# A 64-step stretch of a fused attention and ELU feed-forward kernel: all three engines put in program order, and five instead of three early groups

## The chip, the cores and the metric

The kernel runs on one core of a Trainium2 chip. The metric is device time in microseconds (us) of one execution. The profile is of one execution of its own, by the hardware profiler; its times are microseconds from the start of its span.

## What is computed

Four batches of channel attention over 6080 rows and 256 channels, followed by a feed-forward layer with an ELU over all 24320 rows. Both weights come as 64-bit floats.

```python
def _attn_ref(q, k, v, tau):                       # B, N, C = 4, 6080, 256
    qn = q / (np.linalg.norm(q, axis=1, keepdims=True) + 1e-06)
    kn = k / (np.linalg.norm(k, axis=1, keepdims=True) + 1e-06)
    s = kn.transpose(0, 2, 1) @ qn / tau
    s = s - s.max(-1, keepdims=True)
    a = np.exp(s)
    a /= a.sum(-1, keepdims=True) + 1e-09
    return (v @ a).astype(np.float32)

def _moe_ref(x, w_in, w_out):                      # x: 24320 x 256, d_ff 2048
    h = x @ w_in
    g = np.where(h > 0.0, h, np.exp(np.minimum(h, 0.0)) - 1.0)
    return (g @ w_out).astype(np.float32)
```

## The kernel before

**Stages.** The attention matrix of a batch is only 256 x 256, so the kernel multiplies it into `w_in` first: `wp` = a x `w_in`, kept as a rounded part (hi) and a remainder (lo), and then works on v alone. For batch 0, q and k are read in 24 groups of two rows for each of 128 partitions; TensorE sums their product (`gram`, in full 32-bit precision), ScalarE squares them and VectorE adds the squares (`acc`). Then come the norms (`norms0`, the tile `pn`), the spread of one norm over the partitions (`dg`, a matmul), the softmax, the transposes (`pt`, `aT`) and the projection (`pw`, then `wp`) of the first quarter of `w_in`, in two halves of 256 columns for each of two channel tiles.

**Steps.** After that the kernel goes through steps. A step is one chunk of 512 rows of v (`vt`, or `scr_r` for chunks 2 and 3) and one block of 128 of the 2048 hidden columns. Step i computes `ph`, six matmuls of 512 columns (three for each of two channel tiles: hi x hi, hi x lo, lo x hi); ScalarE makes relu and exp of it, VectorE the ELU (`e`); one step later ScalarE casts it to `g` and VectorE takes the remainder; three steps later six matmuls add it into the output (`po`). The first 64 steps take chunks 0 to 3 in turns of four blocks, so that a quarter of the weights is enough to begin: while they run, the rest of `w_in` and `w_out` is converted from 64-bit floats and the rest of `wp` is projected. After step 64 each chunk has its 16 steps in a row, and the gram products of batches 1 to 3 stand between the output matmuls of these steps, in hi and lo parts.

**Conversion.** `to_f32` is a generator that turns a piece of 64-bit weights into 32-bit ones: one ScalarE operation (Abs) and six on VectorE, with a yield after nearly each. `converting_w_in` does so for `w_in` (into `wf`), `converting_w_out` for `w_out` (into `cv`, then a ScalarE cast and a VectorE remainder into `wo`). A table of steps (`convert`, the list `loose`) says at which step each piece between two yields is issued; `splits` says at which steps the two halves of a chunk of v are cast and split (the list `side`).

**Early groups.** The first `EARLY` = 3 groups of batch 1 are loaded ahead and their gram product is summed in full precision into the PSUM tile `pe` while the softmax of batch 0 runs (`early_items`); the later pass over batch 1 leaves their product out.

**Order.** A scheduler sets the order of each engine's instructions by priorities, but not inside `manual_schedule`, where the named engines take them as the program is written. Before, that holds for TensorE and the DMA queue of SP up to the first step, and for VectorE in the steps up to 66 (64 and three more). ScalarE's order is the scheduler's throughout, and so is TensorE's in the steps. Three PSUM buffers (`w`) go round among `pn`, `pt`, `pw` and `ph`, so a new one waits until the third before it has been read.

## Time and profile before

| what | value |
|---|---|
| median of 3 runs | 2177.08 us (2177.03 to 2178.02) |
| the profiled execution | 2178.38 us, of it the profiled span 2176.6 us |
| TensorE busy | 2165.8 us, 10220 records |
| VectorE busy | 1524.3 us, 2354 records |
| ScalarE busy | 1468.8 us, 2416 records |

A busy time is the sum of an engine's records. TensorE's records overlap one another, so that a full-looking TensorE can still be waiting between two starts; what it loses is read from the starts. A full-precision matmul shows as two records.

### The profile page before, as it was taken

What the parts mean: (1) busy time and instruction counts of PE and PEld (TensorE: products, weight loads), DVE (VectorE), ACT (ScalarE), POOL (GpSimd) and SP (SyncE); (2) the same over time, 40 slices, a digit from 0 to 9 for tenths busy, and PEclk for the clock granted to TensorE, in tenths of its full rate; (3) what the DMA queues carried; (4) which work ended last, traced back from release to release, by engine and by line L of the source; (5) the groups of instructions that cost most, each with busy time, mean ns of one, the idle gap of its engine ahead of it and who ended that gap; (6) DMA issues with size and microseconds to landing.
All of it is one profiled execution on the core that took longest, in us unless ns stands there. A gap on an engine that the chain in (4) does not pass through costs nothing.

```text
span 2176.6 us, 27102 instructions
## 1 busy us (share of the span) xinstructions
PE 2165.8 (100%) x10220; PEld 1907.5 (88%) x10220; DVE 1524.3 (70%) x2354; ACT 1468.8 (67%) x2416; POOL 3.3 (0%) x11
## 2 busy tenths in 40 slices
PE   9999999999999999999999999999999999999999
PEld 8788888898888888889888888888988888888998
DVE  6887777777866777667776667676777666666665
ACT  6876776766767666666676666666676666666665
POOL 0000000000000000000000000000000000000000
PEclk9999999999999999999999999999999999999999
DMA  9310222221201111111021111121112000000000
GB/s 336 126 59 20 78 68 68 68 66 49 61 27 59 59 49 59 49 58 55 30 68 39 49 49 59 49 67 49 46 39 67 21 20 29 29 20 10 20 10 20
DMA packets 61956, 119.73 MB, mean 55 GB/s; under 512 B 6144, under 2 KB 16000, under 8 KB 61824
## 3 DMA queue, kind: packets, MB, share of 16 engines
q1 hardware_dynamic: 61680, 117.86, 16.4%
q8 instruction: 80, 1.31, 0.3%
q14 instruction: 52, 0.43, 0.1%
q10 hardware_dynamic: 144, 0.13, 0.0%
HBM read 90.96 MB, written 27.00 MB: 54 GB/s over the span
## 4 chain that ended last, share of the span: by engine, by line
PE 97%; DVE 1%; ACT 1%; DMA 0%; issue 0%; SPq 0%; DVEq 0%
PE po L431 15%; PE po L433 15%; PE po L429 15%; PE ph L391 15%; PE ph L392 15%; PE ph L393 15%; PE gram L203 3%; PE gram L517 2%; PE gram L210 1%; PE pw L349 0%; PE pw L351 0%; PE pw L350 0%; PE pw L346 0%; ACT e L403 0%; DMA wi<-in_moe_w_in_dram 0%
## 5 line engine op out<-in xcount | busy, mean ns | idle before, releaser
L112 ACT CAST g<-e 128x512 fp32r<-128x512 f32 (+1 forms) x768 | 470.3, 613 | 521.5 <-DVE e L408 285.1
L113 DVE TENSOR_TENSOR g<-e,g 128x512 fp32r<-128x512 f32 (+1 forms) x768 | 525.5, 684 | 325.8 <-ACT g L112 293.1
L429 PE MATMUL po<-g,wo 128*128 128x512 f32 (+1 forms) x1536 | 578.9, 377 | 0.7 <-ACT wo L489 0.7
L431 PE MATMUL po<-g,wo 128*128 128x512 f32 (+1 forms) x1536 | 579.3, 377 | 0.0
L433 PE MATMUL po<-g,wo 128*128 128x512 f32 (+1 forms) x1536 | 577.5, 377 | 0.0
L391 PE MATMUL ph<-vt,wp 128*128 128x512 f32 (+1 forms) x1472 | 556.5, 378 | 1.5 <-DVE e L404 1.5
L392 PE MATMUL ph<-vt,wp 128*128 128x512 f32 (+1 forms) x1472 | 554.6, 377 | 0.1
L393 PE MATMUL ph<-vt,wp 128*128 128x512 f32 (+1 forms) x1472 | 554.5, 377 | 0.0
L404 DVE SCALAR_TENSOR_TENSOR e<-e,ph 128x512 f32<-128x512 f32 (+1 forms) x416 | 283.4, 681 | 251.5 <-ACT e L403 250.1
L429 PEld LDWEIGHTS po<-g,wo 128*128 128x128 f32 x1536 | 290.2, 189 | 39.1 <-ACT wo L489 1.1
L431 PEld LDWEIGHTS po<-g,wo 128*128 128x128 f32 x1536 | 290.3, 189 | 38.1 <-DVE wo L491 0.4
L433 PEld LDWEIGHTS po<-g,wo 128*128 128x128 f32 x1536 | 290.4, 189 | 34.8 <-DVE g L113 0.5
L402 ACT ACTIVATE e<-ph 128x512 f32<-128x512 f32 (+1 forms) x416 | 246.3, 592 | 98.6 <-PE ph L393 83.4
L391 PEld LDWEIGHTS ph<-vt,wp 128*128 128x128 f32 x1472 | 278.2, 189 | 39.6 <-DVE e L404 3.1
L392 PEld LDWEIGHTS ph<-vt,wp 128*128 128x128 f32 x1472 | 278.2, 189 | 36.9 <-issue 0.5
L393 PEld LDWEIGHTS ph<-vt,wp 128*128 128x128 f32 x1472 | 278.2, 189 | 36.0
L403 ACT ACTIVATE e<-e 128x512 f32<-128x512 f32 (+1 forms) x416 | 260.9, 627 | 12.2
L408 DVE TENSOR_TENSOR e<-ph,e 128x512 f32<-128x512 f32 (+1 forms) x352 | 240.9, 685 | 10.4
L406 ACT ACTIVATE e<-ph 128x512 f32<-128x512 f32 (+1 forms) x352 | 207.7, 590 | 30.8 <-PE ph L393 27.3
L407 DVE TENSOR_SCALAR e<-e 128x512 f32<-128x512 f32 (+1 forms) x352 | 147.2, 418 | 21.2 <-ACT e L406 20.9
L182 DVE TENSOR_TENSOR acc<-acc,sq 128x1024 f32<-128x1024 f32 x84 | 102.6, 1221 | 12.6 <-ACT sq L181 11.5
L203 PE MATMUL gram<-qk 128*128 128x512 f32 x276 | 104.6, 379 | 0.0
(120 smaller groups left out, 1170.4 us busy)
## 6 DMA issues: line engine op xcount, KB each, us to landing
raw<-in_q_dram SPq DMA_DIRECT2D x76, 256.0 KB, 2.7
raw<-in_k_dram SPq DMA_DIRECT2D x76, 256.0 KB, 2.9
v<-in_v_dram SPq DMA_DIRECT2D x32, 512.0 KB, 3.6
out_dram<-o SPq DMA_DIRECT2D x56, 256.0 KB, 2.0
v<-in_v_dram SPq DMA_DIRECT2D x16, 496.0 KB, 3.6
out_dram<-o SPq DMA_DIRECT2D x31, 248.0 KB, 2.1
wraw<-w_scr SPq DMA_DIRECT2D x12, 512.0 KB, 3.2
room<-in_q_dram SPq DMA_DIRECT2D x16, 256.0 KB, 5.2
```

The lines of the kernel that those rows point to most:

```text
L112: nc.scalar.copy(hi, src)
L113: nc.vector.tensor_sub(lo, src, hi.bitcast(F32))
L391: nc.tensor.matmul(ph[:, 0:n], wp[kt][:, 0, fs], hi, start=(kt == 0), stop=False)
L392: nc.tensor.matmul(ph[:, 0:n], wp[kt][:, 0, fs], lo, start=False, stop=False)
L393: nc.tensor.matmul(ph[:, 0:n], wp[kt][:, 1, fs], hi, start=False, stop=(kt == KT - 1))
L402: nc.scalar.activation(ev, pv, AF.Relu, scale=-1.0)
L403: x = nc.scalar.activation(ev, ev, AF.Exp, scale=-1.0)
L404: y = nc.vector.scalar_tensor_tensor(ev, ev, -1.0, pv, op0=ALU.add, op1=ALU.max)
L408: y = nc.vector.tensor_tensor(ev, pv, ev, op=ALU.max)
L429: nc.tensor.matmul(o, wo[:, f, 0, ds], hi, start=first(c, f), stop=False)
L431: nc.tensor.matmul(o, wo[:, f, 1, ds], hi, start=False, stop=False)
L433: nc.tensor.matmul(o, wo[:, f, 0, ds], lo, start=False, stop=last(c, f))
```

## The change

1. `EARLY` goes from 3 to 5. Group 3 lies in the fourth quarter of the scratch tile, group 4 in a `raw` buffer of its own; both are loaded on SP's queue between the second load of v and the second load of `w_in`. Their matmuls are not issued before the first step but inside steps 0, 1 and 2, and the copy of `pe` moves to step 3.
2. VectorE is in program order from the norms on, with conversions issued at fixed places in the norms and in the softmax (`meanwhile`); ScalarE from the transposes on. In the softmax of batch 0 ScalarE, not VectorE, scales the gram product.
3. The conversions of the first four rows of `w_out`, and the cast of chunk 1, are spread over the four projections and the first five steps.
4. The first 67 steps run in program order on TensorE and ScalarE as well as VectorE. The tables of conversions and splits change; `converting_w_out` yields once more, so its last piece comes a step later at one place.

```diff
     LEFT = N - RP * P
-    EARLY = 3
+    EARLY = 5
...
-    def inverse_norms(y, ry, squares):
+    def inverse_norms(y, ry, squares, meanwhile=None):
         root = nc.scalar.activation(y, squares, AF.Sqrt)
+        if meanwhile is not None:
+            meanwhile()
         nc.vector.tensor_scalar(ry, y, 1e-30, None, op0=ALU.max)
...
-    def softmax(b, gram, rq, rk, nm):
         for ct in range(KT):
             r = rk[:, ct : ct + 1]
             if b == 0:
-                nc.vector.tensor_scalar(a[:, ct], gram[ct][:, 0, :], r, None, op0=ALU.mult)
+                nc.scalar.activation(a[:, ct], gram[ct][:, 0, :], AF.Copy, scale=r)
...
+        if meanwhile is not None:
+            meanwhile()
         nc.vector.tensor_scalar(sm, sm, 1e-9, None, op0=ALU.add)
         done = nc.vector.reciprocal(sm, sm)
...
+    def split_v_hi(c, raw, vt, kt):
+        n = span(c)[2]
+        nc.scalar.copy(vt[:, kt, 0, 0:n], raw[:, kt, 0:n])
+
+    def split_v_lo(c, raw, vt, kt):
+        n = span(c)[2]
+        nc.vector.tensor_sub(vt[:, kt, 1, 0:n], raw[:, kt, 0:n], vt[:, kt, 0, 0:n].bitcast(F32))
+
     def split_v(c, raw, vt, kt):
-        n = span(c)[2]
-        split(vt[:, kt, 0, 0:n], vt[:, kt, 1, 0:n], raw[:, kt, 0:n])
+        split_v_hi(c, raw, vt, kt)
+        split_v_lo(c, raw, vt, kt)
...
     def converting_w_out(t, n):
-        for of in to_f32(wo64[t // FS][:, t % FS : t % FS + n].rearrange("p t (d x) -> p t d x", x=2)):
-            if of is None:
-                yield
+        if t % FS == 0:
+            state["cv"] = work.tile([P, FS, D], F32, tag="cv", bufs=1, name="cv")
+        ts = slice(t % FS, t % FS + n)
+        of = state["cv"][:, ts]
+        yield from to_f32(wo64[t // FS][:, ts].rearrange("p t (d x) -> p t d x", x=2), of)
         nc.scalar.copy(wo[:, t : t + n, 0], of)
         yield
         nc.vector.tensor_sub(wo[:, t : t + n, 1], of, wo[:, t : t + n, 0].bitcast(F32))
...
-        raw1 = [scratch(x, k=2 * 2).rearrange("p (t r) c -> p t r c", t=2) for x in range(EARLY)]
+        raw1 = [scratch(x, k=2 * 2).rearrange("p (t r) c -> p t r c", t=2) for x in range(M)]
...
         vraw[0] = load_v(0)
-        for x in range(EARLY):
+        for x in range(EARLY - 2):
             fill_rows(raw1[x], 1, x)
         wo64[0] = load_w_out(0)
+        parts = [converting_w_in(0, slice(x * CH // 2, (x + 1) * CH // 2)) for x in range(2)]
+
+        def go_on(part, n):
+            for _ in range(n):
+                next(part, None)
+
         for x in range(FULL - BEHIND, FULL):
             if x == FULL - 2:
-                pn, dg, rk, nm = norms0(acc)
-                with tc.issue_after(summed[0]), tc.issue_after(summed[1]):
-                    at_once(converting_w_in(0, slice(0, CH // 2)))
+                with tc.issue_after(summed[0]), tc.issue_after(summed[1]), tc.manual_schedule(engines={nc.vector.engine}):
+                    go_on(parts[0], 1)
+                    pn, dg, rk, nm = norms0(acc, lambda: go_on(parts[0], 1))
+                    go_on(parts[0], 2)
             gram0_item(x)
         pe = ps.tile([P, KT, C], F32, tag="o", bufs=8 - KT - WB, name="pe")
         spread(pn, dg)
         vraw[1] = load_v(1)
+        raw1.append(work.tile([P, 2, 2, C], F32, tag="raw", bufs=5, name="raw_early"))
+        for x in range(EARLY - 2, EARLY):
+            fill_rows(raw1[x], 1, x)
         wi64[1] = load_w_in(1)
         wo64[1] = load_w_out(1)
-        a0, rs0, attended = softmax(0, pg0, pn[:, 1, :], rk, nm)
-        vts[0] = new_vt(0)
-        with tc.issue_after(attended):
+        wps[0] = new_wp(0)
+        first_w_out, second_w_out = converting_w_out(0, 2), converting_w_out(2, 2)
+
+        def meanwhile():
+            go_on(parts[0], 2)
+            go_on(parts[1], 2)
+
+        with tc.manual_schedule(engines={nc.vector.engine}):
+            a0, rs0, attended = softmax(0, pg0, pn[:, 1, :], rk, nm, meanwhile)
+            vts[0], vts[1] = new_vt(0), new_vt(1)
+            at_once(parts[1])
             for kt in range(KT):
                 split_v(0, vraw[0], vts[0], kt)
             del vraw[0]
-        early_items(4)
-        wps[0] = new_wp(0)
-        aT0, copied = transpose_a(0, a0)
-        attended = (attended, copied)
-        early_items(2 * EARLY - 4)
-        for part in range(2):
-            for ct in range(KT):
-                wp_item(aT0, rs0, wf[0], wps[0], ct, 0, part, 2)
+            early_items(4)
+            with tc.manual_schedule(engines={nc.scalar.engine}):
+                aT0, copied = transpose_a(0, a0)
+                go_on(first_w_out, 2)
+                early_items(2)
+                attended = (attended, copied)
+
+                between = [
+                    lambda: (split_v_hi(1, vraw[1], vts[1], 0), go_on(first_w_out, 1)),
+                    lambda: (split_v_hi(1, vraw[1], vts[1], 1), go_on(first_w_out, 1)),
+                    lambda: (go_on(second_w_out, 1), go_on(first_w_out, 1)),
+                    lambda: go_on(first_w_out, 1),
+                ]
+                for part in range(2):
+                    for ct in range(KT):
+                        wp_item(aT0, rs0, wf[0], wps[0], ct, 0, part, 2)
+                        between[part * KT + ct]()
     nc.sync.dma_start(w_scr[0], wf[0])
     vraw[2] = load_v(2)
-    with tc.issue_after(attended[0]), tc.issue_after(attended[1]):
-        with tc.manual_schedule(engines={nc.vector.engine}):
-            at_once(converting_w_out(0, 2))
-        nc.scalar.copy(early, pe)
...
-    convert(converting_w_out(2, 2), (1, 2, 3, 3, 4, 4, 4), (wi64, 2, load_w_in))
-    convert(converting_w_in(1), (4, 5, 7, 8, 9, 10), (wi64, 3, load_w_in))
-    convert(converting_w_out(4, 4), (11, 12, 13, 14, 15, 16, 17), (wo64, 2, load_w_out))
+
+    for step, n in ((0, 2), (1, 1), (2, 1)):
+        at(step, lambda n=n: early_items(n), True)
+    at(3, lambda: nc.scalar.copy(early, pe), True)
+    convert(first_w_out, (0, 0))
+    convert(second_w_out, (1, 2, 2, 3, 3, 4, 4), (wi64, 2, load_w_in))
+    convert(converting_w_in(1), (1, 5, 6, 8, 8, 10), (wi64, 3, load_w_in))
+    convert(converting_w_out(4, 4), (11, 12, 13, 14, 15, 16, 17, 18), (wo64, 2, load_w_out))
     convert(converting_w_in(2), (18, 19, 20, 21, 22, 23), (wo64, 3, load_w_out))
-    convert(converting_w_out(8, 4), (23, 24, 25, 27, 28, 31, 32))
+    convert(converting_w_out(8, 4), (23, 24, 25, 27, 28, 31, 32, 33))
     convert(converting_w_in(3), (32, 33, 34, 35, 36, 37))
-    convert(converting_w_out(12, 4), (38, 39, 40, 41, 43, 44, 47))
+    convert(converting_w_out(12, 4), (38, 39, 40, 41, 43, 44, 45, 47))
...
-    splits = [(1, 1, 2), (2, 6, 6), (3, 9, 11)]
+    splits = [(1, 0, 1), (2, 5, 7), (3, 9, 11)]
     def prep(x, kt):
         c = splits[x][0]
-        if kt == 0:
-            vts[c] = new_vt(c)
-        split_v(c, vraw[c], vts[c], kt)
+        if c == 1:
+            split_v_lo(c, vraw[c], vts[c], kt)
+        else:
+            if kt == 0:
+                vts[c] = new_vt(c)
+            split_v(c, vraw[c], vts[c], kt)
...
     done = []
-    with tc.manual_schedule(engines={nc.vector.engine}):
+    with tc.manual_schedule(engines={nc.tensor.engine, nc.vector.engine, nc.scalar.engine}):
         for i in range(M * FT + LAG):
             take(i)
```

VectorE between the softmax and the first step. The rows lead from the second half of `wf_0` to the `wp` remainders of two of the four projections; `cv` belongs to `w_out`. Before:

```order
L133 SCALAR_TENSOR_TENSOR wf_0_340<-wi64_0_237,wf_0_340 128x2x256
L129 TENSOR_SCALAR cv_438<-cv_438 128x512
L138 TENSOR_SCALAR cv_s_382<-wf_0_340 128x512
L131 TENSOR_SCALAR cv_438<-cv_438 128x512
L141 SCALAR_TENSOR_TENSOR cv_s_382<-wi64_0_237,cv_s_382 128x512
L133 SCALAR_TENSOR_TENSOR cv_438<-wo64_0_304,cv_438 128x512
L143 TENSOR_TENSOR wf_0_340<-wf_0_340,cv_s_382 128x2x256
L358 SCALAR_TENSOR_TENSOR wp_0_0_398<-pw_412,sums_366,wp_0_0_398 128x256
L358 SCALAR_TENSOR_TENSOR wp_0_1_399<-pw_417,sums_366,wp_0_1_399 128x256
```

And now:

```order
L131 SCALAR_TENSOR_TENSOR wf_0_320<-wi64_0_237,wf_0_320 128x2x256
L136 TENSOR_SCALAR cv_s_395<-wf_0_320 128x512
L139 SCALAR_TENSOR_TENSOR cv_s_395<-wi64_0_237,cv_s_395 128x512
L141 TENSOR_TENSOR wf_0_320<-wf_0_320,cv_s_395 128x2x256
L386 TENSOR_TENSOR vt_0_392<-v_0_296,vt_0_392 128x512 x2
L127 TENSOR_SCALAR cv_421<-cv_421 128x512
L129 TENSOR_SCALAR cv_421<-cv_421 128x512
L360 SCALAR_TENSOR_TENSOR wp_0_0_371<-pw_429,sums_376,wp_0_0_371 128x256
L131 SCALAR_TENSOR_TENSOR cv_421<-wo64_0_304,cv_421 128x512
L360 SCALAR_TENSOR_TENSOR wp_0_1_372<-pw_436,sums_376,wp_0_1_372 128x256
```

The second half of `wf_0` now ends ahead of everything that belongs to `cv`, and the two halves of `vt` stand behind it; the `wp` remainders have conversion pieces of `cv` between them.

VectorE around steps 3 and 4, with the second piece of `w_out` (`cv`) on its way to `wo`. Before:

```order
L133 SCALAR_TENSOR_TENSOR cv_478<-wo64_0_304,cv_478 128x512
L138 TENSOR_SCALAR cv_s_524<-cv_478 128x512
L404 SCALAR_TENSOR_TENSOR e_533<-e_533,ph_526 128x512
L113 TENSOR_TENSOR g_537<-e_508,g_537 128x512
L141 SCALAR_TENSOR_TENSOR cv_s_524<-wo64_0_304,cv_s_524 128x512
L143 TENSOR_TENSOR cv_478<-cv_478,cv_s_524 128x512
L491 TENSOR_TENSOR wo_81<-cv_478,wo_81 128x2x256
```

And now, where `e_530` is step 3 and `e_555` step 4:

```order
L131 SCALAR_TENSOR_TENSOR cv_421<-wo64_0_304,cv_421 128x512
L136 TENSOR_SCALAR cv_s_521<-cv_421 128x512
L414 SCALAR_TENSOR_TENSOR e_530<-e_530,ph_523 128x512
L113 TENSOR_TENSOR g_534<-e_511,g_534 128x512
L139 SCALAR_TENSOR_TENSOR cv_s_521<-wo64_0_304,cv_s_521 128x512
L141 TENSOR_TENSOR cv_421<-cv_421,cv_s_521 128x512
L414 SCALAR_TENSOR_TENSOR e_555<-e_555,ph_548 128x512
L113 TENSOR_TENSOR g_559<-e_530,g_559 128x512
L503 TENSOR_TENSOR wo_81<-cv_421,wo_81 128x2x256
```

The last two pieces of the conversion used to be followed at once by the remainder into `wo`; now a step's `e` and `g` stand between.

ScalarE around step 11, with chunk 3's second half (`scr_r`). Before:

```order
L402 ACTIVATE e_704<-ph_697 128x512
L403 ACTIVATE e_704<-e_704 128x512
L112 CAST g_708<-e_679 128x512
L112 CAST scr_r_86<-v_3_602 128x512
L112 CAST g_736<-e_704 128x512
L127 ACTIVATE wf_3_1216<-wi64_3_695 128x1024
L402 ACTIVATE e_732<-ph_725 128x512
L402 ACTIVATE e_754<-ph_747 128x512
L403 ACTIVATE e_732<-e_732 128x512
```

And now, where the first row is the relu of step 11 and the sixth that of step 12:

```order
L412 ACTIVATE e_722<-ph_715 128x512
L413 ACTIVATE e_722<-e_722 128x512
L112 CAST g_726<-e_697 128x512
L125 ACTIVATE cv_737<-wo64_1_369 128x1024
L382 CAST scr_r_86<-v_3_643 128x512
L412 ACTIVATE e_750<-ph_743 128x512
L413 ACTIVATE e_750<-e_750 128x512
```

The cast of the chunk's half used to follow the cast of `g` at once; now the Abs of the next rows of `w_out` is ahead of it. The conversion of `wf_3`, which stood ahead of two relus, is gone from this place, and relu and exp of a step stand together.

## Rows read from the trace of the kernel before

**Rows 1.** Two stretches: length; busy us of PE, PEld, DVE, ACT, POOL; granted clock; DMA.

```profile
46.00:105.50 59.50, 54.52 (x234) 42.27 (x233) 48.82 (x91) 45.64 (x82) 0.00 (x0) 1.00 0.38 133
105.50:2170.00 2064.50, 2064.45 (x9783) 1825.06 (x9784) 1444.48 (x2234) 1392.54 (x2303) 2.10 (x3) 1.00 0.14 46
```

**Rows 2.** Timeline of TensorE: start, length, line, operation, count, idle before.

```profile
46.03 3.70 PE L517 MATMUL gram<-raw 128*128 128x256 f32 x16
...
50.29 0.70 PE L279 MATMUL pn<-dg,ones 128*128 128x256 f32 x2 [0.56 <-DVE dg L257]
...
60.91 0.57 PE L391 MATMUL ph<-vt,wp 128*128 128x512 f32 x1
...
67.36 0.42 PE L429 MATMUL po<-g,wo 128*128 128x512 f32 x1
...
105.56 0.48 PE L391 MATMUL ph<-scr_r,wp 128*128 128x512 f32 x1 [0.36 <-DVE wp L358]
...
108.25 0.38 PE L391 MATMUL ph<-scr_r,wp 128*128 128x512 f32 x1
...
110.84 0.38 PE L391 MATMUL ph<-scr_r,wp 128*128 128x512 f32 x1
```

**Rows 3.** Timeline of TensorE in the later pass over batch 1.

```profile
285.08 0.38 PE L203 MATMUL gram<-qk 128*128 128x512 f32 x1
285.30 0.38 PE L431 MATMUL po<-g,wo 128*128 128x512 f32 x1
285.51 0.27 PE L210 MATMUL gram<-qk 128*128 128x256 f32 x1
285.62 0.38 PE L433 MATMUL po<-g,wo 128*128 128x512 f32 x1
```

**Rows 4.** Timeline of VectorE ahead of step 0, and one later row.

```profile
51.27 0.74 DVE L300 TENSOR_TENSOR a<-a,pn 128x256 f32<-128x256 f32 x2
...
51.93 0.74 DVE L301 TENSOR_REDUCE nm<-a 128x1 f32<-128x256 f32 x2
...
56.59 0.42 DVE L138 TENSOR_SCALAR cv_s<-wf 128x512 uint32<-128x512 uint32 x1
...
57.26 0.69 DVE L141 SCALAR_TENSOR_TENSOR cv_s<-wi,cv_s 128x512 f32<-128x512 uint32 x1
...
59.06 0.87 DVE L358 SCALAR_TENSOR_TENSOR wp<-pw,sums,wp 128x256 fp32r<-128x256 f32 x2
...
114.86 1.22 DVE L491 TENSOR_TENSOR wo<-cv,wo 128x1024 fp32r<-128x1024 f32 x1
```

**Rows 5.** Timeline of all engines in one step after 106.7 us.

```profile
106.74 0.38 PE L393 MATMUL ph<-scr_r,wp 128*128 128x512 f32 x1
...
107.15 0.60 ACT L402 ACTIVATE e<-ph 128x512 f32<-128x512 f32 x1 [0.41 <-PE ph L393]
...
107.78 0.64 ACT L403 ACTIVATE e<-e 128x512 f32<-128x512 f32 x1
...
108.45 0.69 DVE L404 SCALAR_TENSOR_TENSOR e<-e,ph 128x512 f32<-128x512 f32 x1 [0.49 <-ACT e L403]
...
109.06 0.68 DVE L113 TENSOR_TENSOR g<-e,g 128x512 fp32r<-128x512 f32 x1
```

**Rows 6.** Timeline of ScalarE between 83 and 89 us.

```profile
83.46 1.61 ACT L127 ACTIVATE wf<-wi 128x1024 f32<-128x1024 f32 x1
...
84.95 0.63 ACT L112 CAST g<-e 128x512 fp32r<-128x512 f32 x1
...
87.26 0.63 ACT L403 ACTIVATE e<-e 128x512 f32<-128x512 f32 x1
...
87.80 0.61 ACT L112 CAST g<-e 128x512 fp32r<-128x512 f32 x1
...
88.31 0.61 ACT L112 CAST scr_r<-v 128x512 fp32r<-128x512 f32 x1
```

**Rows 7.** Timeline of SP's DMA queue: the second load of w_in.

```profile
41.39 0.37 SPq L467 DMA_DIRECT2D wi<-in_moe_w_in_dram  x1
```

More of the change, by code (lines that the diff above doesn't have):

```diff
@@ L113, in split, with to_f32 @@
         nc.vector.tensor_sub(lo, src, hi.bitcast(F32))
-    def to_f32(pair, dst=None):
+    def to_f32(pair, dst):
         low, high = pair[:, :, :, 0], pair[:, :, :, 1]
         shape = list(low.shape)
-        if dst is None:
-            dst = work.tile(shape, F32, tag="cv", bufs=1, name="cv")
         af, a = dst, dst.bitcast(U32)
@@ L237, in inverse_norms, with norms0 @@
         return nm
-    def norms0(acc):
+    def norms0(acc, meanwhile):
         pn = ps.tile([P, 2, C], F32, tag="w", bufs=WB, name="pn")
@@ L253, in norms0 @@
         y, ry = (tiny.tile([P, W], F32, name=f"{x}0") for x in ("y", "ry"))
-        nm = inverse_norms(y, ry, pn[:, 0, 0:W])
+        nm = inverse_norms(y, ry, pn[:, 0, 0:W], meanwhile)
         dg = tiny.tile([P, KT, P], F32, tag="y", bufs=1, name="dg")
@@ L279, in spread, with softmax @@
         nc.tensor.matmul(pn[:, 1, :], ones, dg.rearrange("p t j -> p (t j)"), start=True, stop=True)
-    def softmax(b, gram, rq, rk, nm):
+    def softmax(b, gram, rq, rk, nm, meanwhile=None):
         a = work.tile([P, KT, C], F32, tag="a", bufs=1, name=f"a_{b}")
@@ L512, in channel_attention_then_elu_ffn @@
     wi64, wo64, vraw, vts = {}, {}, {}, {}
+    state = {}
     def multiply(raw, r, gram, first, last):
@@ L603, in channel_attention_then_elu_ffn @@
         vraw[1] = load_v(1)
+        raw1.append(work.tile([P, 2, 2, C], F32, tag="raw", bufs=5, name="raw_early"))
+        for x in range(EARLY - 2, EARLY):
+            fill_rows(raw1[x], 1, x)
         wi64[1] = load_w_in(1)
         wo64[1] = load_w_out(1)
-        a0, rs0, attended = softmax(0, pg0, pn[:, 1, :], rk, nm)
-        vts[0] = new_vt(0)
-        with tc.issue_after(attended):
-            at_once(converting_w_in(0, slice(CH // 2, CH)))
+        wps[0] = new_wp(0)
[7 more added lines that the diff above has]
+            at_once(parts[1])
             for kt in range(KT):
@@ L644, in at @@
         (loose if free else side).setdefault(step, []).append(fn)
-    state = {}
     def fetch(w64, x, load):
```

## The prediction, made before the changed kernel ran

> **What bounds the kernel now.** I read the stretches first: busy time of each engine before, in and after the part that the change touches. From 105.50 us to 2170 us TensorE is busy all the time but 0.1 us, at granted clock 1.00 (its upper level, 2.4 GHz), while VectorE and ScalarE are free for 30 to 33% of it [rows 1]. After 105.5 us a removed matmul shortens the run and nothing else does. Before that point TensorE waits. How much is read from starts, not from busy time, because a matmul's record overlaps the next one: the twelve 512-column matmuls of one step take 108.25 to 110.84, so 2.59/12 = 0.2157 us each, though each record shows 0.38 [rows 2]. A full-precision matmul of 256 columns is two such records, 0.43 us: sixteen records last 3.70 us, of which about 0.25 us is the tail of the last, so 3.45 [rows 2].
>
> With these prices I subtract work from time. From 46.03 (the last two groups of batch 0) to 60.91 (the first matmul of step 0) the work is 3.45 for the groups, 0.43 to spread the norms, 3.45 + 1.72 for three early groups, 0.44 for four transposes and 3.45 for four half-width projections: 12.94 of 14.88 us, 1.94 lost. From 60.91 to 67.36 (step 0's output matmul) 24 matmuls, 5.18 of 6.45: 1.27 lost. From 67.36 to 105.56 (step 15) 138 matmuls, 29.77, and four full-precision projections of 0.86, 3.45: 33.2 of 38.2 us, 5.0 lost [rows 2]. So 8.2 us is the most that order can give back, 0.38% of the run.
>
> **The change, term by term.** I write P(i) for the start of the last `ph` matmul of step i.
>
> *More early groups.* Two groups of batch 1 move from the interleaved pass to the early one: eight full-precision matmuls are added, 8 x 0.43 = 3.45 us. Eight of 512 and eight of 256 columns go away from the pass after step 64; there the 512 ones start 0.22 before the next instruction and the 256 ones 0.11 [rows 3], so 4 x 0.216 + 4 x 0.108 = 1.295 per group, **2.59 us off**, in a stretch where TensorE never waits. By themselves the groups cost 0.86 us; they pay only as far as they fill waits. Their four loads of 256 KB stand on SP's queue ahead of the second `wi` load, issued at 41.39 so far [rows 7]; it is first used after step 1, near 66 us. I cost that at nothing; that cover is some ten microseconds.
>
> *Up to step 0.* VectorE now makes the norms without conversions in between, so TensorE no longer waits for `dg`: spread can follow the last gram matmul at about 49.5 and end, as long as its row, near 50.1 (before: 50.29 + 0.70) [rows 2]. The multiply and reduction pairs that took 51.27 to 52.67 [rows 4] end near 51.6; the scaling, moved to ScalarE, lies beside the spread. But VectorE then has a row of conversions ahead of the first `wp` remainder: the end of the first half of `wf`, all of its second half, two remainders of `vt`, two steps of `cv`. They are five of about 0.7, two remainders of 0.6, five short ones of 0.34 to 0.46 and the two tiny ones of `sums` (0.34 for both), by the spacing of the same kinds of rows (0.34 from 56.59 to the next, 0.60 for the long ones, 0.1 more where one needs the one just before) [rows 4]: 7.0 us. So the first `wp` remainder starts at 58.6. It frees the PSUM buffer that the fourth projection needs, at 59.15, and the next remainder, one conversion step later, ends near 60.2 and frees that of step 0. The first step starts at 60.2 instead of 60.91: **0.7 off**.
>
> *Steps 0 to 3.* The early matmuls stand between the `ph` groups: 24 x 0.2157 + 3.45 = 8.63 us to the first `po`, with `e` of step 0 long done. Before it was 6.45: **2.18 on**. The 1.27 lost here is filled.
>
> *Steps 3 to 19, in program order.* The rhythm of one step without backlog [rows 5]: relu starts at P + 0.41, exp at 1.04, `e` on VectorE at 1.71, the remainder of `g` at 2.32, VectorE's next instruction at 2.92. On ScalarE the cast of `g` follows exp by 0.54, the next instruction 0.51 later, and a conversion of 1024 elements holds the engine 1.49 [rows 6]. Four places come too late:
> - Step 8 needs chunk 2's second half, cast at step 7 behind exp and a cast and split by VectorE behind `e` and `g`: the split starts at P(7) + 2.92 and ends 0.69 later; TensorE, at 0.2157 each, would be there after eleven matmuls, at 2.37. Late by 1.28 (0.04 from an end to the release).
> - Step 12 needs chunk 3's second half. On ScalarE a 1024-element conversion of step 11 stands ahead of its cast: P(11) + 1.04 + 0.54 + 0.51 + 1.49 = 3.58, cast and split end at 4.92, TensorE is there at 2.37: 2.59.
> - The output matmul of step 2 needs `wo` rows 2 and 3. From P(1): relu, exp, cast, a 1024-element conversion, then relu of step 2 at 3.58, `e` of step 2 at 4.87; ten VectorE instructions (0.34 to 0.79) to the last remainder at 11.0, end 11.74. TensorE's work in between (46 slots of 0.2157, eight of them early matmuls' records) is 9.92: 1.82.
> - The output matmul of step 16 needs the remainder of `wo` 4 to 7, which the extra yield moves from step 17 to 18: P(18) + 2.92 + 1.22 + 0.04 = 4.18 (1.22 is that remainder's row now [rows 4]) against 14 matmuls, 3.02: 1.16.
>
> Together 6.85 where 5.0 was lost: **1.87 on**. What goes away is every wait that a conversion hoisted ahead of a relu caused; what comes in its place is the latency of a table that issues each split just before its use.
>
> *The rest of the 64 steps.* ScalarE needs 0.63 + 0.54 + 0.51 = 1.7 us of a 2.59 us step, so a 1.49 us conversion leaves 0.6 to carry, gone a step later. An output matmul wants a `g` whose remainder ended at P + 3.0 of the step before, about 2.8 us ahead of need. No cost.
>
> Sum: 2.18 + 1.87 - 0.7 - 2.59 = **+0.8 us**. Bounds: restarts after a wait cost 0.10 (a first record of 0.48 against 0.38 [rows 2]), four of them 0.4, and a ScalarE late by the 0.6 above at two of the four places 1.2; VectorE's long conversions at their bare 0.60 take about 0.8 away, and 0.03 less in each of some twenty links, the spread of such starts, another 0.6. The likeliest is -0.6 to +2.4. The profiled execution took 2178.38, 1.8 us beyond its span of 2176.6; the median of the runs is 2177.08. I put the difference on the median: **2177.8 us**, own range 2176.5 to 2179.5.
>
> **The clock.** The rows grant 1.00 although TensorE lost 8.2 us in short gaps between 46.00 and 105.50 [rows 1], and the changed order has gaps of the same sum and size, so the sum holds. The Trainium skill, TensorE: Matmul & The Clock Gate, section "A second HAM failure mode: psum-queue depth-cycling", says that small idles between matmul groups that cycle through PSUM banks can make the clock flip between its levels. By that rule the steps of the new waits would run at the lower level; no row here shows that level, and the trace does not agree with the rule so far.
>
> **Rivals.**
> 1. *The waits vanish.* If program order lets the three engines run staggered far enough that none of the four late places shows, the sum is 2.18 - 5.0 - 0.7 - 2.59 = -6.1 us, 2171.0. For it: ScalarE and VectorE have room. Against: each chain above is a latency behind TensorE's own matmul, with no backlog in it; a quicker engine doesn't shorten it. 0.07; that half of them show, 2174.4: 0.05.
> 2. *Slower: ScalarE falls behind.* In program order every relu stands behind the conversions of the step before. If the backlog passes 2.8 us, TensorE waits for `g` at each of some five conversions after step 16, at 1.49 each: +0.8 + 7.5, 2185.4. It decides from about two conversions and a pair of copies inside two steps; the table puts one into a step. 0.05.
> 3. *The moved groups don't come back as time.* If the slots of the later pass were filled by a wait, 2.59 is not returned: 2180.4. Against: TensorE's full rows there. 0.03.
> 4. *The clock falls* for 20 us or more: the same matmuls at half the clock take 20 us more, 2198. 0.02.
>
> **The numbers.** The likeliest case has 0.78. A difference under 0.2%, 4.35 us, can hardly be told from none by a measurement of this kernel; between 2172.7 and 2181.4 lie the likeliest case, half of rival 1 and rival 3: same 0.86. Faster 0.07 (rival 1 whole), slower 0.07 (rivals 2 and 4). The range takes in half of rival 1 and rival 3: 2174.2 to 2180.4, 0.86 of the chance.
>
> **What would show it.** Right: step 0 starting near 60.2, the first `po` near 69, TensorE waits of 1 to 2.6 us before steps 8 and 12 for `scr_r` and for `wo` at steps 2 and 16, step 20 about 3.4 us later than now, no wait after, and 16 fewer gram matmuls in the later pass. Wrong: TensorE starts without a gap at those four places, or waits for `g` after step 20.

## The result, and the profile after

| | before | after |
|---|---|---|
| median | 2177.23 us (2176.42 to 2179.41, 22 executions) | 2180.8 us (2178.92 to 2181.62, 22 executions) |
| ratio | 1 | 1.0014, 95% interval 1.0008 to 1.0021 |
| profiled execution, span | 2178.38, 2176.6 us | 2180.8, 2179.0 us |

The ratio means 3.0 us more (1.7 to 4.6), where +0.8 was forecast. The median of 2180.8 is 3.0 over the forecast of 2177.8, 1.3 over the upper end of the likeliest case (2179.5) and 0.4 over that of the wider range (2180.4). The prediction held that less than 0.2% can hardly be told from none; the measured 0.14% can: its interval leaves out 1.

The same two stretches as in [rows 1], after the change:

```profile
46.00:105.50 59.50, 54.41 (x234) 44.45 (x233) 48.12 (x85) 40.47 (x75) 0.00 (x0) 0.97 0.42 144
105.50:2170.00 2064.50, 2063.48 (x9769) 1827.11 (x9769) 1441.14 (x2232) 1392.74 (x2307) 2.10 (x3) 1.00 0.14 46
```

The busy time of TensorE in the first stretch is the same to 0.1 us; what is new is its clock, 0.97 in place of 1.00. Behind 105.5 us 1.02 us is idle that was not.

TensorE's timeline, with the landmarks of [rows 2], every row behind 46 us that begins after an idle time, and four more that are used below (82.01, the start of step 8; 97.18; 102.97, a projection; 233.86, the start of step 60; in this kernel `ph` is L401 to L403, `po` L439 to L443):

```profile
45.21 3.70 PE L530 MATMUL gram<-raw 128*128 128x256 f32 x16
48.74 0.59 PE L279 MATMUL pn<-dg,ones 128*128 128x256 f32 x2
...
58.86 1.13 PE L348 MATMUL pw<-wf,aT 128*128 128x256 f32 x4 [1.20 <-DVE wp L360]
...
59.85 0.48 PE L401 MATMUL ph<-vt,wp 128*128 128x512 f32 x1
...
68.59 0.38 PE L439 MATMUL po<-g,wo 128*128 128x512 f32 x1
...
74.50 0.48 PE L439 MATMUL po<-g,wo 128*128 128x512 f32 x1 [0.57 <-ACT wo L501]
75.65 0.48 PE L441 MATMUL po<-g,wo 128*128 128x512 f32 x1 [0.67 <-DVE wo L503]
...
82.01 0.38 PE L401 MATMUL ph<-scr_r,wp 128*128 128x512 f32 x1
...
83.30 0.48 PE L401 MATMUL ph<-scr_r,wp 128*128 128x512 f32 x1 [0.48 <-ACT scr_r L382]
84.22 0.48 PE L402 MATMUL ph<-scr_r,wp 128*128 128x512 f32 x1 [0.43 <-DVE scr_r L386]
...
96.13 0.48 PE L401 MATMUL ph<-scr_r,wp 128*128 128x512 f32 x1 [1.51 <-ACT scr_r L382]
96.86 0.48 PE L402 MATMUL ph<-scr_r,wp 128*128 128x512 f32 x1 [0.24 <-DVE scr_r L386]
97.18 0.49 PE L403 MATMUL ph<-scr_r,wp 128*128 128x512 f32 x1
...
102.97 1.88 PE L348 MATMUL pw<-wf,aT 128*128 128x512 f32 x4
...
122.05 0.48 PE L441 MATMUL po<-g,wo 128*128 128x512 f32 x1 [1.02 <-DVE wo L503]
...
233.86 0.38 PE L401 MATMUL ph<-scr_r,wp 128*128 128x512 f32 x1
```

All seven idle times behind step 0 stand at the four places that the prediction named: step 2's output (74.50), steps 8 and 12, step 16's output (122.05). In the kernel before, step 60 starts at 229.07:

```profile
229.07 0.38 PE L391 MATMUL ph<-scr_r,wp 128*128 128x512 f32 x1
```

The idle times add up to 4.92 us, but that is not what the waits cost. A row's idle time counts from the end of the record ahead, 0.38 long, while TensorE starts a matmul every 0.2157; that hides 0.164. And the first record after a wait is 0.48 long, 0.10 more. So each wait costs 0.264 more than its bracket says: 4.92 + 7 x 0.264 = 6.77.

Granted clock of the changed kernel around step 12 (columns as in [rows 1]):

```profile
94.00:96.00 2.00, 0.63 (x3) 0.20 (x2) 1.29 (x2) 2.00 (x4) 0.00 (x0) 1.00 0.76 311
96.00:98.00 2.00, 1.62 (x5) 1.12 (x6) 0.69 (x1) 0.37 (x2) 0.00 (x0) 0.83 0.00 0
98.00:100.00 2.00, 2.00 (x6) 1.58 (x5) 1.00 (x2) 1.44 (x3) 0.00 (x0) 0.50 0.00 0
100.00:102.00 2.00, 2.00 (x9) 1.73 (x8) 1.59 (x3) 0.12 (x1) 0.00 (x0) 0.82 0.00 0
```

Right behind the longest wait the clock falls to its lower level (0.50, 1.2 GHz), and TensorE does six matmuls in 2 us instead of nine. From the L403 record behind the wait to the projection of that step (97.18 to 102.97) it takes 5.79 us; the same instructions at full clock in another kernel below (e2) take 4.10. The fall costs 1.69 us. Two more profiles with a fall at this place, e5 and e12, also take 5.79.

For the comparisons I cut the run at four starts of TensorE: A, the last sixteen `gram` matmuls; B, step 0; C, the first `po`; D, step 60. A itself lies between 44.5 and 46.4 us in kernels whose program up to there is the same, so only the pieces behind it are compared. From C to D every one of these traces has the same 702 TensorE records, so that piece is the same work in another order. From B to C the early matmuls differ: no record of them in before and e5, 12 in e6, e8, e10 and e11, where one item (four records, 0.86 us) stands ahead of B, and 16 in the others. The last column says whether the clock fell in the profiled execution (in its last microseconds it falls in every trace).

| kernel | A to B | B to C | C to D | D to the end | clock fell |
|---|---|---|---|---|---|
| before | 14.88 | 6.45 | 161.71 | 1947.53 | no |
| after | 14.64 | 8.74 | 165.27 | 1945.14 | yes |
| e1 step 12 alone | 14.65 | 8.74 | 161.23 | 1945.14 | no |
| e2 step 8 alone | 14.66 | 8.74 | 162.32 | 1945.11 | no |
| e3 step 16 alone | 14.66 | 8.73 | 162.23 | 1945.13 | no |
| e12 step 2 alone | 14.64 | 8.74 | 164.03 | 1945.16 | yes |
| e4 all four | 14.64 | 8.74 | 156.80 | 1945.18 | no |
| e7 e4 with step 12 late again | 14.64 | 8.74 | 159.58 | 1945.12 | no |
| e8 e4 with a filled wait | 14.64 | 7.87 | 156.80 | 1945.12 | no |
| e5 three early groups | 14.64 | 5.28 | 167.27 | 1947.55 | yes |
| e6 ACT, PE by scheduler | 14.65 | 7.88 | 159.63 | 1945.42 | no |
| e9 ACT by scheduler | 14.65 | 8.73 | 165.31 | 1945.16 | no |
| e10 PE by scheduler | 16.34 | 7.88 | 159.53 | 1945.10 | yes, behind A |
| e11 e4 by scheduler | 14.64 | 7.88 | 158.53 | 1945.18 | no |

After less before, in the spans: A -0.82, A to B -0.24, B to C +2.29, C to D +3.56 (of it 1.69 the clock), D to the end -2.39; sum +2.40, and 2179.0 - 2176.6 is 2.4.

### The profile page after: what moved, and what is told of

Read it like the earlier page. It is cut to its first block, busy times and chain, and to the rows that moved or that the text cites. A ratio compares the mean times of both kernels' runs of the same rounds, so it can differ in the third digit from the quotient of the medians.

```text
span 2179.0 us, 27167 instructions
## 1 busy us (share of the span) xinstructions
PE 2167.0 (99%) x10220; PEld 1914.2 (88%) x10220; DVE 1521.9 (70%) x2350; ACT 1465.8 (67%) x2416; POOL 3.3 (0%) x11
## 4 chain that ended last, share of the span: by engine, by line
PE 98%; DVE 1%; ACT 1%; issue 0%; DMA 0%; SPq 0%; DVEq 0%; ACTq 0%
PE po L441 15%; PE po L443 15%; PE ph L401 15%; PE ph L402 15%; PE po L439 15%; PE ph L403 15%; PE gram L201 3%; PE gram L530 2%; PE gram L208 1%; PE pw L348 1%; PE pw L353 0%; PE pw L351 0%; PE pw L352 0%; ACT e L412 0%; DVE g L113 0%
## 5 line engine op out<-in xcount | busy, mean ns | idle before, releaser
L439 PE MATMUL po<-g,wo 128*128 128x512 f32 (+1 forms) x1536 | 580.1, 378 | 0.6 <-ACT wo L501 0.6
L443 PE MATMUL po<-g,wo 128*128 128x512 f32 (+1 forms) x1536 | 579.4, 378 | 0.0
L401 PE MATMUL ph<-vt,wp 128*128 128x512 f32 (+1 forms) x1472 | 557.5, 379 | 0.0
L403 PE MATMUL ph<-vt,wp 128*128 128x512 f32 (+1 forms) x1472 | 555.2, 377 | 0.0
L439 PEld LDWEIGHTS po<-g,wo 128*128 128x128 f32 x1536 | 291.1, 190 | 38.2 <-ACT wo L501 1.0
L443 PEld LDWEIGHTS po<-g,wo 128*128 128x128 f32 x1536 | 291.6, 190 | 33.9
L401 PEld LDWEIGHTS ph<-vt,wp 128*128 128x128 f32 x1472 | 278.9, 189 | 36.8 <-DVE e L414 0.8
L403 PEld LDWEIGHTS ph<-vt,wp 128*128 128x128 f32 x1472 | 278.9, 189 | 35.4
```

The costliest lines, as they stand in the source:

```text
L401: nc.tensor.matmul(ph[:, 0:n], wp[kt][:, 0, fs], hi, start=(kt == 0), stop=False)
L403: nc.tensor.matmul(ph[:, 0:n], wp[kt][:, 1, fs], hi, start=False, stop=(kt == KT - 1))
L439: nc.tensor.matmul(o, wo[:, f, 0, ds], hi, start=first(c, f), stop=False)
L443: nc.tensor.matmul(o, wo[:, f, 0, ds], lo, start=False, stop=last(c, f))
```

## Experiments

All edits are made in the changed kernel unless it says otherwise. Theory: each late place is a latency of its own, set by the table of steps, and the clock fell because of the wait before step 12. Rivals: the engines are behind as a whole, so a wait taken away shows up at the next place; the clock falls for another reason.

### One late place at a time

**e1**, step 12:

```diff
-    splits = [(1, 0, 1), (2, 5, 7), (3, 9, 11)]
+    splits = [(1, 0, 1), (2, 5, 7), (3, 9, 10)]
```

> One entry of the changed kernel's table moves: the second half of chunk 3 is cast and split at step 10 instead of 11, so its cast stands ahead of the 1024-element conversion. In the changed kernel's trace TensorE waits 1.51 + 0.24 us before step 12 and right behind it runs 3.4 us at half clock, which costs 1.7. Theory (the wait is the latency of this one place, and the clock fell because of it): both go, the first ph of step 60 comes near 230.3 instead of 233.86, the time is 2180.8 - 3.5 = 2177.3, and no half clock is left. Rival A (the clock falls from the row of waits before, not from this one): the wait goes, the clock falls all the same, 2179.0. Rival B (ScalarE and VectorE are behind as a whole): the wait shows at the next place, the output matmul of step 16, which waits 2 us or more instead of 1.02, and the time stays above 2180.

2176.51 us, ratio to before 0.9997 (0.9988 to 1.0006). C to D is 4.04 shorter: 1.69 of the clock and 2.35 for the wait. The only wait left behind step 8 is the one for `wo`, no longer than before:

```profile
117.75 0.48 PE L441 MATMUL po<-g,wo 128*128 128x512 f32 x1 [1.02 <-DVE wo L503]
```

Neither rival holds. The mean granted clock of each execution is on record too: it is under 1.000 in 18 of 22 executions of the changed kernel (median of these 2181.0, of the other four 2179.2) and in none of 11 here.

**e2**, step 8:

```diff
-    splits = [(1, 0, 1), (2, 5, 7), (3, 9, 11)]
+    splits = [(1, 0, 1), (2, 5, 6), (3, 9, 11)]
```

> One entry moves: the second half of chunk 2 is cast and split at step 6 instead of 7. In the changed kernel TensorE waits 0.48 + 0.43 us before step 8. Theory (each late place is its own latency): these go, the wait before step 12 stays at 1.5 to 2.0 and the half clock behind it stays; step 60 near 232.9, time 2179.8. Rival A (the clock falls when waits pile up, this one among them): the half clock goes as well, 2178.1. Rival B (backlog): the time stays at 2180.8, with the 0.9 us added to the wait before step 12.

2178.95 us, ratio 1.0007 (0.9997 to 1.0016). Without the clock, C to D is 163.58 - 162.32 = 1.26 shorter. The wait before step 12 is unchanged, but the clock did not fall behind it in this profile; by the mean clock it fell in 4 of 11 executions:

```profile
96.05 0.48 PE L401 MATMUL ph<-scr_r,wp 128*128 128x512 f32 x1 [1.51 <-ACT scr_r L382]
96.78 0.48 PE L402 MATMUL ph<-scr_r,wp 128*128 128x512 f32 x1 [0.24 <-DVE scr_r L386]
97.10 0.38 PE L403 MATMUL ph<-scr_r,wp 128*128 128x512 f32 x1
...
101.20 1.88 PE L348 MATMUL pw<-wf,aT 128*128 128x512 f32 x4
```

The latency theory holds; my expectation that the lower clock stays as a fixed price does not. Rival A (the waits pile up, and this one is among the causes) is left open by the 4 of 11; e7 below bears on it.

**e3**, step 16:

```diff
-    convert(converting_w_out(4, 4), (11, 12, 13, 14, 15, 16, 17, 18), (wo64, 2, load_w_out))
+    convert(converting_w_out(4, 4), (11, 12, 13, 14, 15, 16, 17, 17), (wo64, 2, load_w_out))
```

> One entry moves: the remainder of output weight rows 4 to 7 is issued at step 17 again instead of 18. In the changed kernel TensorE waits 1.02 us for it. Theory: this wait goes and nothing else, the waits before steps 8 and 12 and the half clock stay; step 60 near 232.8, time 2179.7. Rival (backlog): VectorE is then late with the next pieces, TensorE waits elsewhere behind step 16, and the time stays at 2180.8.

2179.16 us, ratio 1.0006 (0.9998 to 1.0015). The wait goes and nothing comes in its place: 163.58 - 162.23 = 1.35. The clock fell in 6 of 11 executions, not in the profiled one.

**e12**, step 2:

```diff
-    convert(second_w_out, (1, 2, 2, 3, 3, 4, 4), (wi64, 2, load_w_in))
+    convert(second_w_out, (0, 1, 1, 2, 2, 3, 3), (wi64, 2, load_w_in))
```

> One table line of the changed kernel moves: the second output-weight piece (rows 2 and 3) is issued a step earlier throughout, at steps 0, 1, 1, 2, 2, 3, 3. In the changed kernel the output matmul of step 2 waits 0.57 + 0.67 for it. Theory (a latency of its own, 1.82 from start to start by the forecast; the other three places gave 2.33, 1.23 and 1.33 of the 6.77 that all four gave, which leaves 1.88): this wait goes, the first ph of step 8 starts 1.8 to 1.9 earlier counted from step 0; steps 8, 12 and 16 wait as before, up to 0.5 more at step 8 because VectorE's pieces now meet there; time 2178.9 with the half clock in most executions, 2177.5 without. Rival (backlog): the 1.9 shows again in full at step 8, 2180.8.

2178.53 us, ratio 1.0004 (0.9995 to 1.0013); the clock fell in 4 of 11 executions. From step 0 to step 8 it takes 79.57 - 59.17 = 20.40 instead of 82.01 - 59.85 = 22.16: 1.76 shorter. Of that 0.53 is lost again at step 8, as expected (0.96 in place of 0.43):

```profile
79.57 0.38 PE L401 MATMUL ph<-scr_r,wp 128*128 128x512 f32 x1
...
80.86 0.48 PE L401 MATMUL ph<-scr_r,wp 128*128 128x512 f32 x1 [0.48 <-ACT scr_r L382]
82.30 0.48 PE L402 MATMUL ph<-scr_r,wp 128*128 128x512 f32 x1 [0.96 <-DVE scr_r L386]
```

### All four places, and one of them back

**e4**:

```diff
-    convert(second_w_out, (1, 2, 2, 3, 3, 4, 4), (wi64, 2, load_w_in))
-    convert(converting_w_in(1), (1, 5, 6, 8, 8, 10), (wi64, 3, load_w_in))
-    convert(converting_w_out(4, 4), (11, 12, 13, 14, 15, 16, 17, 18), (wo64, 2, load_w_out))
+    convert(second_w_out, (0, 1, 1, 2, 2, 3, 3), (wi64, 2, load_w_in))
+    convert(converting_w_in(1), (6, 6, 7, 9, 10, 11), (wi64, 3, load_w_in))
+    convert(converting_w_out(4, 4), (11, 12, 13, 14, 14, 15, 16, 16), (wo64, 2, load_w_out))
...
-    splits = [(1, 0, 1), (2, 5, 7), (3, 9, 11)]
+    splits = [(1, 0, 1), (2, 4, 5), (3, 8, 9)]
```

> Program order on all three engines and five early groups stay; only the tables change: chunk 2 is cast and split at steps 4 and 5, chunk 3 at 8 and 9, the second output-weight piece one step earlier throughout (steps 0 to 3), the second input-weight quarter at steps 6 to 11, the third output-weight piece ends at step 16. Theory: all four late places vanish, 1.24 + 0.91 + 1.75 + 1.02 = 4.9 us with 0.4 of restarts, and the half clock with its 1.7: step 60 near 226.9, time 2180.8 - 7.0 = 2173.8, 0.15% under the kernel before. Rival A (clock falls without the waits): 2175.5. Rival B (ScalarE and VectorE cannot take the pieces in fewer steps): waits of the same sum for g, 2178 to 2181.

2172.36 us, ratio 0.9976 (0.9966 to 0.9986). TensorE's row has no idle time from step 0 on, at full clock (length; busy; clock):

```profile
46.00:60.00 14.00, 12.80 (x61) 10.57 (x60) 12.12 (x32) 8.33 (x19) 0.00 (x0) 1.00 0.71 248
60.00:130.00 70.00, 70.00 (x318) 59.84 (x318) 61.66 (x90) 58.84 (x99) 0.00 (x0) 1.00 0.30 103
```

C to D is 163.58 - 156.80 = 6.78 shorter without the clock. The single places gave 2.35, 1.26, 1.35 and 1.76, sum 6.72: they are independent to within 0.1 us. Program order with these tables is no bound; VectorE and ScalarE take the pieces in fewer steps.

**e7** puts one late place back into e4: `(3, 8, 11)` in `splits`.

> The kernel with the new tables (2172.4, no wait after step 0), with one late place put back: the second half of chunk 3 is cast and split at step 11, behind the 1024-element conversion. Both theories: TensorE waits 1.5 + 0.2 before step 12, which costs 2.3 from start to start, 2174.7. Theory A (this wait alone brings the half clock, in a part of the executions): some executions with a mean clock of 0.999, 1.7 longer than the others. Theory B (it takes the waits before it as well): all executions at 1.000.

2176.29 us, ratio 0.9997 (0.9988 to 1.0005). C to D is 2.78 longer, for two waits that sum to 2.26:

```profile
94.04 0.48 PE L401 MATMUL ph<-scr_r,wp 128*128 128x512 f32 x1 [1.52 <-ACT scr_r L382]
95.27 0.48 PE L402 MATMUL ph<-scr_r,wp 128*128 128x512 f32 x1 [0.74 <-DVE scr_r L386]
```

The mean clock was under 1.000 in 7 of 11 executions (median 2177.1 us, of the other four 2175.2). Theory A: waits at this one place, with none elsewhere behind step 0, are enough for the lower clock. No trace of e7 shows where it fell; in e4, without them, it fell in none of 8. The wait itself was forecast at 2.3; with e4's tables a conversion of 1.22 us stands on VectorE right ahead of the split, so the remainder comes 0.5 later.

### The two groups

**e5**: `EARLY = 3`, the loads and early items of groups 3 and 4 taken out.

> The changed kernel with three early groups again: no matmuls of groups 3 and 4 in steps 0 to 2, their 16 matmuls back in the later pass; everything else stays. Theory (the two groups fill part of the waits): the four early items and three changes of matmul type go, 3.45 + 0.54, but the output matmul of step 2 then waits some 1.3 more for its weights and the ones before it some 0.6 for g, so step 60 comes about 2.0 earlier counted from the last sixteen gram matmuls, and behind step 60 the run takes 2.39 more: +0.4, 2181.2 with the half clock behind step 12, 2179.6 without it. Rival A (the groups are pure cost in the early part): 1.6 faster than the changed kernel. Rival B (they lie wholly in waits): 2.4 slower.

2182.58 us, ratio 1.0025 (1.0014 to 1.0035). B to C is 3.46 shorter, which is their eight matmuls at 0.43; C to D is 2.00 longer, because step 2's output now waits 1.89 where it waited 0.57:

```profile
72.47 0.48 PE L439 MATMUL po<-g,wo 128*128 128x512 f32 x1 [1.89 <-ACT wo L501]
```

D to the end is 2.41 longer. So the groups gain 2.00 + 2.41 - 3.46 = 0.95 in this kernel, and both rivals fall in the trace. The medians show 5.6 over before against 3.6 for the changed kernel, 2.0 apart, which is as near to rival B (2.4). The clock can carry part of that: it was under 1.000 in 7 of 8 executions, and in three of them, the longest three (2183.3 to 2184.1), the mean was 0.998, about what two falls make (an estimate: 2 x 1.69 of 2180 is 0.16%); no execution of the changed kernel has 0.998. No trace shows a second fall, so what the groups are worth beyond 0.95 stays open.

**e8**, on top of e4:

```diff
-                    lambda: (go_on(second_w_out, 1), go_on(first_w_out, 1)),
+                    lambda: (go_on(second_w_out, 1), go_on(first_w_out, 1), early_items(1)),
...
-    for step, n in ((0, 2), (1, 1), (2, 1)):
+    for step, n in ((1, 3),):
...
-    at(3, lambda: nc.scalar.copy(early, pe), True)
+    at(2, lambda: nc.scalar.copy(early, pe), True)
```

> The kernel with the new tables, and of the four early items that stand in steps 0 to 2 one moves between the third and the fourth projection, where TensorE waits 1.20, and the other three stand together in step 1. Theory: 0.86 of the wait is filled and step 0 starts no later; one change from full-precision to rounded matmuls in place of three saves 2 x 0.18; 2172.4 - 1.2 = 2171.2, no wait after step 0. Rival (a wait for PSUM or e comes back in step 0 to 2, where the items stood): 2172.4 or more.

2171.71 us, ratio 0.9974 (0.9963 to 0.9985). The wait before the fourth projection shrinks from 1.20 to 0.34, and B to C by 0.87:

```profile
59.22 1.13 PE L348 MATMUL pw<-wf,aT 128*128 128x256 f32 x4 [0.34 <-DVE wp L360]
```

That is the 0.86 of the filled wait alone, and it is read from the two traces: the medians put e8 and e4 both 5.3 us under the kernel before. The 0.36 for fewer changes of matmul type is not there. I had read it from rows: the first rounded matmul after full-precision ones is 0.57 long and the next comes 0.40 later, not 0.2157. But four full-precision ones ahead take only 1.54 from start to start (61.25 to 62.79 in the changed kernel), not 1.73. The two cancel.

### Which engine's program order

**e6**, **e9**, **e10** change one line, the engines in program order during the steps: VectorE alone; VectorE and TensorE; VectorE and ScalarE. The rest is left to the scheduler.

```diff
-    with tc.manual_schedule(engines={nc.tensor.engine, nc.vector.engine, nc.scalar.engine}):
+    with tc.manual_schedule(engines={nc.vector.engine}):
```

> The changed kernel with ScalarE's and TensorE's order in the 67 steps left to the scheduler again, VectorE's by the program, tables and groups as changed. Theory (program order only changes where the waits stand, the table of steps decides how many): the waits before steps 8 and 12 for scr_r shrink, others for g and for PSUM behind hoisted conversions come back, the sum within 1.5 of the changed kernel's 6.8, time 2178 to 2181. Rival (program order itself made the waits): most of them vanish, 2175 or less.

2174.94 us, ratio 0.9989 (0.9980 to 0.9998). My theory fell: with the tables of the change and the scheduler's order the run is faster than before, by 2.1 us in the medians. So it is the program order on TensorE and ScalarE, and not the rest of the change, that makes the changed kernel slower. C to D is 3.95 shorter than after without the clock, B to C 0.86 (the scheduler puts an early item into the wait before the fourth projection). Its TensorE at step 8:

```profile
80.83 0.38 PE L403 MATMUL ph<-scr_r,wp 128*128 128x512 f32 x1
81.04 0.38 PE L439 MATMUL po<-g,wo 128*128 128x512 f32 x1
81.26 0.38 PE L441 MATMUL po<-g,wo 128*128 128x512 f32 x1
82.24 0.48 PE L401 MATMUL ph<-scr_r,wp 128*128 128x512 f32 x1 [0.60 <-ACT scr_r L382]
82.56 0.38 PE L443 MATMUL po<-g,wo 128*128 128x512 f32 x1
82.78 0.38 PE L439 MATMUL po<-g,wo 128*128 128x512 f32 x1
82.99 0.38 PE L441 MATMUL po<-g,wo 128*128 128x512 f32 x1
83.21 0.38 PE L443 MATMUL po<-g,wo 128*128 128x512 f32 x1
83.42 0.38 PE L401 MATMUL ph<-scr_r,wp 128*128 128x512 f32 x1
83.64 0.38 PE L402 MATMUL ph<-scr_r,wp 128*128 128x512 f32 x1
```

Two output matmuls stand ahead of the `ph` matmul that needs the late cast (82.24), and four between it and the one that needs the late remainder (83.64), which then waits for nothing.

> The changed kernel with TensorE and VectorE in program order and only ScalarE left to the scheduler. With both left to it the run was 4.8 us shorter up to step 60 than the changed kernel without the half clock. Theory T (TensorE's order made the difference: the scheduler puts two to nine output matmuls between the halves of a late ph, so the late half is covered): program order on TensorE takes that away, the waits before steps 8 and 12 stay at 1 us or more each, 2178 or more. Theory S (ScalarE's order made it: the scheduler takes the casts of v ahead of the 1024-element conversions): the waits before steps 8 and 12 stay small, 2175.

2181.54 us, ratio 1.0020 (1.0011 to 1.0030). C to D is 165.31, 1.73 more than after without the clock. The waits before step 8 are longer than after, those before step 12 are 0.91 and 0.93:

```profile
84.63 0.48 PE L401 MATMUL ph<-scr_r,wp 128*128 128x512 f32 x1 [1.43 <-ACT scr_r L382]
86.37 0.48 PE L402 MATMUL ph<-scr_r,wp 128*128 128x512 f32 x1 [1.26 <-DVE scr_r L386]
```

> The other half: ScalarE and VectorE in program order, only TensorE left to the scheduler. Theory T: the late halves of steps 8 and 12 come at the same time as in the changed kernel, but output matmuls stand ahead of them and cover them, 2175 or a little less, no half clock. Theory S: the cast of chunk 3 stands behind the long conversion again, so TensorE waits 1.5 before step 12 as in the changed kernel, 2178 to 2181.

2174.49 us, ratio 0.9986 (0.9977 to 0.9995). C to D 159.53 and B to C 7.88, as in e6: TensorE's order made the whole difference (theory T). Of the waits before steps 8 and 12 one of 0.77 is left, before step 12. ScalarE's order is worth 0.1 beside a scheduled TensorE, and 1.7 in favour of the program's beside a TensorE in program order (e9).

**e11**: the line of e6 in e4.

> The new tables (2172.4 in program order), with ScalarE and TensorE left to the scheduler. Theory (with no late place the order has nothing to cover; the scheduler also moves an early item into the wait before the fourth projection, 0.86): 2171.5. Rival (the scheduler hoists a 1024-element conversion ahead of an exp or a cast of g, as in the kernel before): waits of 1 to 5 us come back for g between steps 6 and 16, 2173 to 2177.

2173.31 us, ratio 0.9981 (0.9972 to 0.9989). Between the two: 0.86 is filled before step 0, and 1.73 is lost again in C to D, among others for a remainder of `g` and one of `wp`:

```profile
83.82 0.48 PE L443 MATMUL po<-g,wo 128*128 128x512 f32 x1 [0.39 <-DVE g L113]
105.97 0.48 PE L403 MATMUL ph<-scr_r,wp 128*128 128x512 f32 x1 [0.58 <-DVE wp L360]
```

With tables in which nothing is late, program order on all three engines is the faster one by the traces: from B to the end e4 takes 0.87 less than e11, and e8 1.80 less. The ratios point the same way, though their intervals overlap. e4 and e8 have the lowest times of all, both 5.3 us under the kernel before measured beside them, and beat both kernels.

## Why the prediction was right in its places and 3 us too low

- **Up to step 0** (forecast -0.7, measured -0.24). `dg` is out of the way as foreseen: spread starts 3.53 behind A instead of 4.26. The step that failed is "the multiply and reduction pairs end near 51.6". I set the pairs right behind the spread's end and laid the scaling on ScalarE beside it at no cost; the pairs start 0.52 behind that end, 1.11 behind the spread's start, and take 1.58 instead of 1.40. The profile puts the wait down to the scaling (L291), but the scaling ended at 49.42, 0.43 before the first pair, so what held the pairs stays open. In [rows 2, 4] they start 0.98 behind the spread's start, but there VectorE itself was scaling just before. ScalarE and VectorE after the change, then VectorE before it:

```profile
48.51 0.91 ACT L291 ACTIVATE a<-gram,rk 128x256 f32<-128x256 f32 x2 [0.41 <-PE gram L530]
...
49.85 0.42 DVE L300 TENSOR_TENSOR a<-a,pn 128x256 f32<-128x256 f32 x1 [1.22 <-ACT a L291]
...
51.43 0.68 DVE L139 SCALAR_TENSOR_TENSOR cv_s<-wi,cv_s 128x512 f32<-128x512 uint32 x1
...
58.33 0.48 DVE L360 SCALAR_TENSOR_TENSOR wp<-pw,sums,wp 128x256 fp32r<-128x256 f32 x1
```

```profile
50.48 0.88 DVE L291 TENSOR_SCALAR a<-gram,rk 128x256 f32<-128x256 f32 x2
```

  From 51.43 to 58.33 is 6.90; the row of conversions was forecast at 7.0. Only its start was wrong: 51.43 is 6.22 behind A, and 51.6 with A at 46.03 was 5.57.
- **Steps 0 to 3** (+2.18): +2.29. Right.
- **The four late places** (6.85 in place of 5.0, +1.87): 6.78 in place of 161.71 - 156.80 = 4.91, +1.87. One by one, step 8 1.26 (forecast 1.28), step 12 2.35 (2.59), step 2 1.76 (1.82), step 16 1.35 (1.16). Mechanism, places and sizes hold, and rival 1 with them falls; that the +1.87 is met to 0.01 is luck, step 12 came out 0.24 under its forecast and step 16 0.19 over. But the reason given was half of it: "a table that issues each split just before its use". TensorE's own program order, which keeps the six output matmuls behind all six `ph` matmuls, turns the late operands into waits of that size; with the scheduler's order on TensorE, C to D is 163.58 - 159.53 = 4.05 shorter (e10). The prediction treated program order on TensorE as free.
- **The later pass** (-2.59): -2.39 from step 60 on, in e5 2.41, for 16 gram matmuls fewer (536 after 552). Right in kind, 0.2 too much; rival 3 falls.
- **The rest of the 64 steps** (no cost): no idle row between 122.05 and step 60, and e4 runs them with still closer tables. Right, and none of the idle rows waits for `g`; rival 2 falls.
- **The clock.** This is the term that failed: "the changed order has gaps of the same sum and size, so the sum holds." The sum of the gaps was the wrong thing to compare. No single gap between 50 and 106 us was longer than 0.96 before (the row below); the forecast itself put 2.59 at one place. By its mean in each execution, the clock fell in 18 of 22; in the profiled one it fell right behind that wait, at a cost of 1.69. Rival 4 had the mechanism, but only with 20 us. The Trainium skill, TensorE: Matmul & The Clock Gate, section "A second HAM failure mode: psum-queue depth-cycling", blames frequent small idles; e7 shows the lower clock with waits at one place alone, and before, with many small ones, had it in 2 of 98 executions (those timed beside the experiments).

```profile
59.30 1.97 PE L346 MATMUL pw<-wf,aT 128*128 128x256 f32 x8 [0.96 <-DVE wf L143]
```

The sum in the profile, +2.40, differs from the forecast +0.8 by the clock 1.69, step 0 0.46, the later pass 0.20 and steps 0 to 3 0.11, less the 0.82 by which A came earlier in this one execution: 1.64. Over 22 executions each, A should average out (no trace shows it): the medians lie 3.0 (by the ratio) to 3.6 above before.

**What stays open.** Why the same waits before step 12 bring the lower clock in 18 of 22 executions of the changed kernel but in 14 of 33 of e2, e3 and e12, which run the same program from step 9 to step 15. Chance alone would split such counts so unevenly in under one of a hundred cases, but the groups were chosen after the counts were seen, and the kernels were timed on different chips (e2 and e3 on one, e12 on another), so a difference between chips is not excluded. That each of the other waits adds to the chance is a third reading; e7, 7 of 11 with all of them gone, speaks against it, but its waits at step 12 are 0.5 longer.

## What to carry to other kernels

Before an engine is put in program order, look for work that the scheduler's order puts between a late operand and the engine that waits for it. With TensorE in program order each operand has to be ready by its place in the code, so its table entry must lie a whole chain ahead (here two to three steps instead of one): then program order is the best of all by the traces (e8), otherwise it costs more than it gives (e10 against after). Price the longest single wait for the clock as well as for itself. And take a wait's cost from start to start: the bracket in the timeline left out 0.26 us of each.
